# Zero-padded k heads and full-height score products, and a state sum on VectorE, in a linear-attention and MLP kernel

## The chip, the cores and the metric

One core of a Trainium2 chip runs the whole program. The engines are TensorE (PE, the matrix products; PEld is its weight load), VectorE (DVE), ScalarE (ACT), GpSimd (POOL) and SyncE (SP, which here only issues transfers). TensorE writes to PSUM[...]; VectorE and ScalarE read it from there. Everything else lies in SBUF, 128 partitions wide. Times are device microseconds of this core; the metric is the median of the runs.

## The reference

Four batches, 8 heads, 768 steps, head size 48. First a recurrent attention with a decay w per channel and a bonus u for the step itself, then an MLP with a norm and a residual:

```python
for t in range(S):
    cur = einsum('bhd,bhe->bhde', u * kt, vt)
    y[:, :, t] = einsum('bhd,bhde->bhe', rt, state + cur)
    state = w[..., None] * state + einsum('bhd,bhe->bhde', kt, vt)
x  = y as (B, S, H*D)                                   # 384 wide
xn = (x - mean) / sqrt(var + 1e-6) * g_ln
out = x + relu(xn @ w_ch1) @ w_ch2                      # 384 -> 1536 -> 384
```

## The kernel before

Each sequence of 768 steps is cut into six chunks of 128, so that there are 24 chunks, 6 to a batch, numbered 0 to 23. Within a chunk the recurrence is turned into products: k and r are scaled by powers of w (`scale_k`, line 359, and `scale_r`, line 362), k and r are transposed on TensorE (lines 377 and 392), and masked scores times v give the output of the chunk, to which the product of r with the state before the chunk is added. Heads are kept in pairs: a pair takes 128 partitions of a transposed tile, 64 to a head, of which 48 carry values and 16 are zeros.

For chunk i the steps are, with the planner's names:

- `TK` and `TR` transpose k and r into the PSUM bank `tr`, of which there is one (r for two chunks at a time). `kT` (line 381) and `rT` (line 398) copy them to SBUF as bf16, on ScalarE or VectorE.
- `q` (line 405) is the product of rT and kT for the bonus; `cc` (line 433) sums it over a head by four narrow matmuls into the last columns of the bank `s`; `cp` (line 444) copies the result, and `Vb` (line 448) multiplies v by it on GpSimd.
- `at` (line 412) is the scores: eight matmuls, one for each head, over 48 partitions, which begin at partition 0 for an even head and at 64 for an odd one. `A` (line 423) multiplies by the mask, in two instructions on VectorE that read PSUM.
- `kv` makes the new state in the bank `s`: an identity product adds the decayed state of the chunk before, Z (line 455), and four matmuls add k times v (line 464). `Z` (line 475) multiplies the sum by the decay of a whole chunk, on VectorE from PSUM, and writes bf16.
- `y` (lines 487 and 499) is r times Z and A times v. `x` (line 512) adds the bonus on VectorE, `xn` (line 525) and `sq` (line 532) on ScalarE prepare the norm, and `rs` (lines 538 and 541) on GpSimd makes the factor of the row, which is applied at the very end.
- xn is transposed for the MLP: on TensorE for chunks 0 to 7 (line 563), by DMA, issued on SyncE, for the others (`lc`, line 571).
- `up` (line 588) and `dn` (line 614) are the two MLP products, cut into blocks of some 0.65 us; `re` (line 599) is the relu on ScalarE; `ot` (line 624) finishes the row on VectorE, and `st` (line 635) stores it. The first six chunks go through the MLP singly, the others in pairs.

v comes as f32 and is cast to bf16 (`vc`, line 368) on whichever engine the plan gives it. The weights are scaled or cast once (lines 341, 343 and 353). Before the first down product, and only there, TensorE is kept busy with products of the identity (line 261).

The order of the work is not written out. A planner (`Planner.order`) holds for every step its engine, a cost, the steps it needs, the buffers it takes and gives back, a priority and, for some, other engines with their costs. It plays the program through with these costs, always takes the step that can start first, and picks the engine on which it would be done first. What comes out is a fixed order of instructions for each engine; on the chip each engine works through its own list and waits where an input isn't there. So a change of a cost, or of a buffer count, moves instructions on every engine. The pools are named in the call of the planner: `tr`, `at`, `s`, `y` and `o` are single PSUM banks, `hp` is two, and `x` has NX = 16 buffers in SBUF, each held from `x` to `ot`. Loads of k, v and r go through SyncE in a fixed row, with seven buffers for k and for v and four for r.

Of the kernel before, what the change touches and what calls it, by code (L numbers as in the profile page):

```python
# [9 lines left out]
FP32 = mybir.dt.float32  # L10
BF16 = mybir.dt.bfloat16
ALU = mybir.AluOpType
# [107 lines left out]
def kernel(  # L120
# [12 lines left out]
    nc = tc.nc  # L133
# [6 lines left out]
    DP = P // 2  # L140
# [10 lines left out]
    NX = 16  # L151
# [100 lines left out]
    nc.vector.memset(WLZ[:], 0.0)  # L252
    uwI = const.tile([P, HP, 2], BF16, name="uwI")
# [115 lines left out]

    def k_bank(i):  # L370
        return "y" if i < 1 else "tr"
# [7 lines left out]
    def evacuate_k(i, eng):  # L379
        kT_t[i] = trp.tile([P, HP, P], BF16, name="kT", bufs=NKT)  # L380
        (eng.copy if eng is nc.scalar else eng.tensor_copy)(out=kT_t[i][:], in_=tk_t[i][:, :HP, :])  # L381

# [20 lines left out]
    def product(i, eng):  # L403
        q_t[i] = sb2.tile([P, HP, P], BF16, name="q")
        eng.tensor_tensor(out=q_t[i][:], in0=rT_t[i][:], in1=kT_t[i][:], op=ALU.mult)  # L405

    def scores(i):
        at_t[i] = ps.tile([P, 2, HP, P], FP32, name="at")
        for p in range(HP):
            for par in range(2):  # L410
                p0 = par * DP
                nc.tensor.matmul(  # L412
                    out=at_t[i][:, par, p, :],
                    lhsT=kT_t[i][p0 : p0 + D, p, :],
                    rhs=rT_t[i][p0 : p0 + D, p, :],
                    start=True,
                    stop=True,
                )
# [33 lines left out]
    def state(i):  # L452
        ksc = k_bufs[i % NSC].rearrange("p (q e) d -> p q (e d)", e=2)
        if i % NCH > 0:
            nc.tensor.matmul(
                out=s_t[i][:, : HP * E2],
                lhsT=ident[:],
                rhs=Z_t[i - 1][:].rearrange("p q e -> p (q e)"),
                start=False,
                stop=True,  # L460
                skip_group_check=True,
            )
        for p in range(HP):
            nc.tensor.matmul(
                out=s_t[i][:, p * E2 : (p + 1) * E2],
                lhsT=ksc[:, p, :],
                rhs=v_t[i][:, 2 * p : 2 * p + 2, :],
                start=False,
                stop=True,
                skip_group_check=True,  # L470
            )

# [71 lines left out]
    xT_t, hT_t, o_t, rs_t = {}, {}, {}, {}  # L544
# [9 lines left out]
    KP = 24  # L554
    ot_t = {}
# [77 lines left out]
    def store(i, eng):  # L633
# [6 lines left out]
             Z=3, x=NX, sum=4, sqs=4, sq=2, xn=3, xT=3, hT=NH, ot=3)  # L640
# [42 lines left out]
    for i in range(NT):  # L683
# [17 lines left out]
        if i < KP:  # L701
# [8 lines left out]
        add(f"q{i}", "DVE", 0.45, lambda e, i=i: product(i, e), [f"kT{i}", f"rT{i}"], [("q", i, 1)], [("kT", i)], pri=p0 + 1, alt=[("POOL", 1.15)])  # L710
        add(f"at{i}", "PE", 0.43, lambda i=i: scores(i), [f"kT{i}", f"rT{i}"], [("at", i, 2)], [("kT", i)], pri=p0 + 1)
# [8 lines left out]
        if not last:  # L720
            z = [f"Z{i - 1}"] if c else []
            add(f"kv{i}", "PE", 0.36 if c else 0.2, lambda i=i: state(i), [f"cc{i}", f"vc{i}", f"sck{i}"] + z, [],
                [("sck", i), ("vv", i)] + ([("Z", i - 1)] if c else []), pri=p0 + 1)
            add(f"Z{i}", "DVE", 0.57, lambda i=i: decay(i), [f"kv{i}", "WLZ"],
                [("Z", i, 2 if c < NCH - 2 else 1)], [("s", i)], pri=p0)
# [35 lines left out]
    for t in plan.order():  # L761
# [5 lines left out]
        if t["fn"] is not None:  # L767
            if t["alt"]:
                t["fn"]({"ACT": nc.scalar, "DVE": nc.vector, "POOL": nc.gpsimd, "SP": nc.sync}[t["eng"]])
            else:  # L770
                t["fn"]()
# [28 lines left out]
```

## Time and profile before

| | |
|---|---|
| median of 6 runs | 163.03 us (162.03 to 164.77) |
| the profiled execution's time | 162.03 us |
| its span, first to last instruction | 160.0 us |
| first down product | 28.96 us |
| last x of the attention (line 512) | 121.16 us |
| TensorE busy | 149.6 us |
| VectorE busy | 108.6 us |
| ScalarE busy | 103.0 us |
| GpSimd busy | 87.0 us |
| input and output moved | 25.46 MB |

The span is 2.0 us shorter than the execution's time, and the profiled execution is the fastest of the six. Busy times are of one execution; an engine can be busy and still not set the end. In the lists of instructions, "x8" is eight equal instructions that follow each other, with the time from the start of the first to the end of the last; for TensorE that includes the time a product needs to run through, so that the next one starts before the printed end.

### The profile page before, as it was taken

The numbers are of one execution on the slowest core, as the hardware profiler recorded it, in microseconds if no ns is written. First come the engines' busy times: TensorE is split into PE (matmuls) and PEld (weight loads), VectorE is DVE, ScalarE is ACT, GpSimd is POOL, SyncE is SP. The second block draws the span as 40 slices with busy tenths as digits, with TensorE's granted clock in tenths as the row PEclk, the third lists the DMA queues.
The fourth block names the chain that finished last, engine by engine and source line by source line (L and its number), as shares of the span: only waits on it lengthen the run. The fifth ranks groups of instructions, "written<-read, shape, count | busy, mean of one in ns | idle before, by whom it ended". The sixth has DMA issues, their size and how long they took to land.

```text
span 160.0 us, 4708 instructions
## 1 busy us (share of the span) xinstructions
PE 149.6 (93%) x1875; PEld 117.1 (73%) x1875; DVE 108.6 (68%) x234; ACT 103.0 (64%) x234; POOL 87.0 (54%) x133
## 2 busy tenths in 40 slices
PE   5999999999999989999996979999999999999990
PEld 5788798787788757778874757878677777777550
DVE  5889997799887969889967967878693111111331
ACT  3575898788788697597929569676767554542000
POOL 7379897767489699969786943844152000000000
PEclk9999999999999999999999999999999999999998
DMA  4999999999999798999999862121121221101222
GB/s 101 222 229 333 346 197 296 360 209 233 228 232 251 151 256 166 247 236 171 233 163 209 158 161 74 53 63 39 49 49 53 74 74 49 50 3 51 102 104 87
DMA packets 75418, 25.46 MB, mean 159 GB/s; under 512 B 69632, under 2 KB 74246, under 8 KB 75398
## 3 DMA queue, kind: packets, MB, share of 16 engines
q1 hardware_dynamic: 73254, 23.60, 63.5%
q10 hardware_dynamic: 2048, 1.57, 3.0%
q8 instruction: 14, 0.23, 0.6%
q14 instruction: 6, 0.05, 0.1%
q0 software_dynamic: 96, 0.01, 0.0%
HBM read 18.88 MB, written 4.72 MB: 147 GB/s over the span
## 4 chain that ended last, share of the span: by engine, by line
PE 63%; SPq 13%; DMA 8%; ACT 7%; DVE 4%; issue 2%; ACTq 0%
PE hp L588 23%; PE o L614 23%; SPq L188 8%; DMA v<-in_v_dram 4%; DMA wst<-in_moe_w_ch_dram 4%; PE at L412 4%; PE tr L377 3%; SPq L182 2%; PE hp L614 2%; SPq L210 2%; PE tr L392 2%; PE y L499 2%; ACT hT L599 2%; ACT sq L532 2%; DVE A L423 2%
## 5 line engine op out<-in xcount | busy, mean ns | idle before, releaser
L588 PE MATMUL hp<-xT,w_sb 128*128 128x256 bf16 (+1 forms) x540 | 58.3, 251 | 2.9 <-ACT hT L599 1.3
L614 PE MATMUL o<-w_sb,hT 128*128 128x384 bf16 x264 | 52.6, 326 | 0.3 <-DVE ot L624 0.2
L599 ACT ACTIVATE hT<-hp 128x512 bf16<-128x512 f32 x72 | 42.1, 597 | 14.9 <-PE hp L588 13.7
L588 PEld LDWEIGHTS <-w_sb 128*128 128x128 bf16 x540 | 43.5, 98 | 10.4 <-issue 3.0
L614 PEld LDWEIGHTS <-hT 128*128 128x128 bf16 x288 | 26.9, 98 | 13.1 <-DVE w_sb L353 0.3
L624 DVE SCALAR_TENSOR_TENSOR ot<-o,rs,x 128x384 f32<-128x384 f32 x22 | 13.5, 613 | 28.4 <-PE o L614 28.4
L423 DVE TENSOR_TENSOR A<-at,mask 128x512 bf16<-128x512 f32 x48 | 30.7, 681 | 2.5 <-PE at L412 2.5
L448 POOL TENSOR_TENSOR Vb<-v,cc 128x384 f32<-128x384 f32 x24 | 21.4, 891 | 10.0 <-ACT cc L444 9.9
L362 POOL TENSOR_TENSOR sc<-r,Fr 128x384 bf16<-128x384 f32 x16 | 16.6, 1049 | 4.3 <-ACT Fr L303 2.7
L512 DVE SCALAR_TENSOR_TENSOR x<-y,Vb 128x384 f32<-128x384 f32 x24 | 13.2, 552 | 7.1 <-POOL Vb L448 4.9
L525 ACT ACTIVATE xn<-x,sum 128x384 bf16<-128x384 f32 x24 | 14.8, 615 | 4.5 <-DVE x L512 4.5
L359 POOL TENSOR_TENSOR sc<-k,Fk 128x384 bf16<-128x384 f32 x14 | 14.5, 1040 | 1.5 <-DMA k<-in_k_dram 1.3
L532 ACT ACTIVATE sq<-x,sum 128x384 bf16<-128x384 f32 x24 | 14.7, 613 | 0.0
L541 POOL TENSOR_TENSOR rs<-rs,expo 128x1 f32<-128x1 f32 x24 | 13.3, 555 | 2.0
L261 PE MATMUL o<-ident 128*128 128x128 bf16 x164 | 12.6, 232 | 1.6 <-DVE ident L236 1.6
L538 POOL TENSOR_SCALAR rs<-sqs 128x1 f32<-128x1 f32 x24 | 5.5, 231 | 12.9 <-ACT sq L532 9.0
L475 DVE TENSOR_TENSOR Z<-s,WLZ 128x384 bf16<-128x384 f32 x20 | 10.9, 547 | 2.3 <-ACT cc L444 2.3
L368 ACT CAST vv<-v 128x384 bf16<-128x384 f32 x14 | 7.2, 515 | 8.0 <-DMA v<-in_v_dram 8.0
L261 PEld LDWEIGHTS <-ident 128*128 128x128 bf16 x164 | 10.4, 104 | 2.0 <-DVE ident L236 1.6
L398 ACT COPY rT<-tr 128x512 bf16<-128x512 bf16 x12 | 8.6, 734 | 4.3 <-PE tr L392 2.9
L405 DVE TENSOR_TENSOR q<-rT,kT 128x512 bf16<-128x512 bf16 x22 | 10.6, 481 | 0.6 <-ACT kT L381 0.2
L377 PE MATMUL tr<-ident,sc 128*128 128x128 bf16 x92 | 8.9, 219 | 1.5 <-DVE rT L398 1.1
(81 smaller groups left out, 192.8 us busy)
## 6 DMA issues: line engine op xcount, KB each, us to landing
r<-in_r_dram SPq DMA_DIRECT2D x12, 384.0 KB, 4.8
k<-in_k_dram SPq DMA_DIRECT2D x24, 192.0 KB, 4.5
wst<-in_moe_w_ch_dram SPq DMA_DIRECT2D x6, 768.0 KB, 7.4
v<-in_v_dram SPq DMA_DIRECT2D x23, 192.0 KB, 3.9
out_dram<-ot SPq DMA_DIRECT2D x17, 192.0 KB, 2.0
out_dram<-ot ACTq DMA_DIRECT2D x7, 192.0 KB, 1.9
xT<-xn SPq DMA_TRANSPOSE x16, 3.0
v<-in_v_dram ACTq DMA_DIRECT2D x1, 192.0 KB, 3.8
```

Source lines behind the costliest of these rows:

```text
L261: nc.tensor.matmul(out=warm[:, :P], lhsT=ident[:], rhs=ident[:], start=True, stop=True)
L359: eng.tensor_tensor(out=k_bufs[i % NSC][:, :, :D], in0=k_t[i][:], in1=Fk[:], op=ALU.mult)
L362: eng.tensor_tensor(out=r_bufs[e % NSR][:, j, :, :D], in0=r_t[e][:, :, j * D : (j + 1) * D], in1=Fr[:, j], op=ALU.mult)
L377: nc.tensor.transpose(out=tk_t[i][:, q, :], in_=sc[:, q, :], identity=ident[:])
L423: nc.vector.tensor_tensor(out=A_t[i][:, par], in0=at_t[i][:, par], in1=mask[:].unsqueeze(1).to_broadcast([P, HP, P]), op=ALU.mult,)
L448: nc.gpsimd.tensor_tensor(out=Vb_t[i][:], in0=vf_t[i][:], in1=cc_t[i][:].unsqueeze(2).to_broadcast([P, H, D]), op=ALU.mult)
L525: nc.scalar.activation(out=xn_t[i][:], in_=x_t[i][:], func=ACT.Identity, bias=sum_t[i][:], scale=-float(C))
L532: nc.scalar.activation(out=sq[:], in_=x_t[i][:], func=ACT.Square, bias=sum_t[i][:], scale=-float(C), accum_out=sq_t[i][:])
L588: nc.tensor.matmul(out=hp[:, f * gw : (f + 1) * gw], lhsT=w1_sb[:, n, kc, fb * P : (fb + 1) * P], rhs=xT_t[g][:, kc, :gw], start=(kc == 0) ...
L599: nc.scalar.activation(out=hT_t[g][:, nf * m : nf * (m + 1), :gw], in_=hp_t[g, m][:].rearrange("p (f t) -> p f t", f=nf), func=ACT.Relu,)
L614: nc.tensor.matmul(out=o_t[i][:, :C], lhsT=hT_t[g][:, fk, j * P : (j + 1) * P], rhs=w2_sb[:, fk, :], start=(fk == 0), stop=(fk == FK - 1),)
L624: nc.vector.scalar_tensor_tensor(out=ot_t[i][:], in0=o_t[i][:, :C], scalar=rs_t[i][:], in1=x_t[i][:], op0=ALU.mult, op1=ALU.add,)
```

## The change

From chunk 8 on (KZ = 8) k is no longer copied to one SBUF tile. Three buffers of twice the size (kz) are zeroed once by GpSimd, and two copies, one for the even heads and one for the odd, put each head of k into its own 128-partition column, with zeros in the other head's half. The scores of these chunks are eight products over all 128 partitions. q reads k from the PSUM bank, which is given back only when both copies and q are done.

From chunk 6 on (SZ = 6), for chunks that are neither the first nor the last of their batch, the identity product is left out. VectorE adds the decayed state before to the k times v sum in PSUM and writes f32 (S, two buffers), and a second instruction multiplies this by the decay, on GpSimd or on VectorE as the planner picks. NX goes from 16 to 11. The planner's cost of the unpadded scores is 0.56 instead of 0.43.

```diff
-    NX = 16
+    NX = 11
@@
+    NKZ = 3
+    kz_bufs = []
+    for i in range(NKZ):
+        t_ = const.tile([P, HP, 2, P], BF16, name=f"kz{i}")
+        for par in range(2):
+            nc.gpsimd.memset(t_[(1 - par) * DP : (2 - par) * DP, :, par, :], 0.0)
+        kz_bufs.append(t_)
@@
+    def wide(i):
+        return KZ <= i < KP
@@
+    def spread_k(i, par, eng):
+        p0 = par * DP
+        (eng.copy if eng is nc.scalar else eng.tensor_copy)(
+            out=kz_bufs[i % NKZ][p0 : p0 + DP, :, par, :], in_=tk_t[i][p0 : p0 + DP, :HP, :]
+        )
@@ def product(i, eng):
-        eng.tensor_tensor(out=q_t[i][:], in0=rT_t[i][:], in1=kT_t[i][:], op=ALU.mult)
+        kT = tk_t[i][:, :HP, :] if wide(i) else kT_t[i][:]
+        eng.tensor_tensor(out=q_t[i][:], in0=rT_t[i][:], in1=kT, op=ALU.mult)
@@ def scores(i):
+        if wide(i):
+            for p in range(HP):
+                for par in range(2):
+                    nc.tensor.matmul(
+                        out=at_t[i][:, par, p, :],
+                        lhsT=kz_bufs[i % NKZ][:, p, par, :],
+                        rhs=rT_t[i][:, p, :],
+                        start=True,
+                        stop=True,
+                    )
+            return
@@ def state(i):
-        if i % NCH > 0:
+        if i % NCH > 0 and not apart(i):
@@
+    def apart(i):
+        return i >= SZ and 0 < i % NCH < NCH - 1
+
+    def add_state(i):
+        sum_s[i] = sb2.tile([P, HP, E2], FP32, name="S")
+        nc.vector.tensor_tensor(
+            out=sum_s[i][:],
+            in0=s_t[i][:, : HP * E2].rearrange("p (q e) -> p q e", q=HP),
+            in1=Z_t[i - 1][:],
+            op=ALU.add,
+        )
+
+    def decay_sum(i, eng):
+        Z_t[i] = sb3.tile([P, HP, E2], BF16, name="Z")
+        eng.tensor_tensor(out=Z_t[i][:], in0=sum_s[i][:], in1=WLZ[:], op=ALU.mult)
@@
+    KZ, SZ = 8, 6
@@ the plan
+        if wide(i):
+            add(f"TK{i}", "PE", 0.24, lambda i=i: transposes_k(i), [f"sck{i}"], [("tr", ("k", i), 3)], [("sck", i)], pri=p0)
+            add(f"kzb{i}", "", 0.0, None, [f"TK{i}"], [("kz", i, 1)], pri=p0)
+            for t in range(2):
+                add(f"kz{i}{t}", "ACT", 0.58, lambda g, i=i, t=t: spread_k(i, t, g), [f"kzb{i}"], [], [("tr", ("k", i))],
+                    pri=p0, alt=[("DVE", 0.45)])
+            add(f"kT{i}", "", 0.0, None, [f"kz{i}0", f"kz{i}1"], pri=p0)
...
+        if wide(i):
+            add(f"q{i}", "DVE", 0.55, lambda e, i=i: product(i, e), [f"TK{i}", f"rT{i}"], [("q", i, 1)], [("tr", ("k", i))],
+                pri=p0 + 1, alt=[])
+            add(f"at{i}", "PE", 0.45, lambda i=i: scores(i), [f"kT{i}", f"rT{i}"], [("at", i, 2)], [("kz", i)], pri=p0 + 1)
...
-        add(f"at{i}", "PE", 0.43, ...)
+            add(f"at{i}", "PE", 0.56, ...)
...
+            if apart(i):
+                add(f"kv{i}", "PE", 0.2, lambda i=i: state(i), [f"cc{i}", f"vc{i}", f"sck{i}"], [],
+                    [("sck", i), ("vv", i)], pri=p0 + 1)
+                add(f"S{i}", "DVE", 0.57, lambda i=i: add_state(i), [f"kv{i}"] + z, [("S", i, 1)],
+                    [("s", i), ("Z", i - 1)], pri=p0)
+                add(f"Z{i}", "POOL", 1.0, lambda e, i=i: decay_sum(i, e), [f"S{i}", "WLZ"],
+                    [("Z", i, 2 if c < NCH - 2 else 1)], [("S", i)], pri=p0 + 2, alt=[("DVE", 0.55)])
```

## The prediction

> **What bounds the kernel now.** I read the page's busy table and its 40 slices first: which engine is full, and where it is not.
>
> ```profile
> PE 149.6 (93%) x1875; PEld 117.1 (73%) x1875; DVE 108.6 (68%) x234; ACT 103.0 (64%) x234; POOL 87.0 (54%) x133
> PE   5999999999999989999996979999999999999990
> DVE  5889997799887969889967967878693111111331
> ACT  3575898788788697597929569676767554542000
> PEclk9999999999999999999999999999999999999998
> DMA  4999999999999798999999862121121221101222
> ```
>
> TensorE is full in nearly every 4 us slice and holds its full clock; the dips are slice 15 (56 to 60 us) and slices 22 and 24 (84 to 88 and 92 to 96 us). Inputs keep the DMA rings near full up to some 88 us. From 122 us on, only the MLP's products are left (DVE at 1). So: loads set the pace to 29 us, then TensorE with holes. To size the holes I costed TensorE's list after the first down product (starts 28.96 us) with start-to-start times from its timeline, because a printed duration there includes the pipeline's depth:
>
> ```profile
> 109.03 0.36 PE L499 MATMUL y<-vv,A 128*128 128x48 bf16 x8
> 109.32 0.40 PE L412 MATMUL at<-rT,kT 48*128 48x128 bf16 x8
> 109.65 0.25 PE L433 MATMUL s<-uwI,q 128*128 128x2 bf16 x4
> 109.76 0.32 PE L455 MATMUL s<-Z,ident 128*128 128x384 bf16 x1
> 109.92 0.33 PE L464 MATMUL s<-vv,sc 128*128 128x96 bf16 x4
> 110.09 0.61 PE L392 MATMUL tr<-ident,sc 128*128 128x128 bf16 x8
> 110.54 0.81 PE L614 MATMUL o<-w_sb,hT 128*128 128x384 bf16 x4
> ```
>
> Scores take 0.33, then bonus 0.11, identity product 0.16, state 0.17, eight full-height transposes 0.45. Before the scores stands a hole: eight y products take 0.20 (as from 49.36 to 49.57), so 109.23 to 109.32 is about 0.10 lost, and the same hole precedes almost every set of scores. A set costs 0.43. With 0.65 for a down or up block, 0.37 for y and 0.22 for a k transpose, 72 down, 65 up, 20 scores, 20 bonus, 13 identity, 16 state, 20 y, 19 k, 9 r and 5 LayerNorm transposes sum to 121.0 us: the end would be 150.0. TensorE really ends at 156.3. **6.3 us are holes**: 0.9 by chunk 7's y, 2.7 by chunk 15's, 4.6 by chunk 17's, 6.0 by chunk 18's, 6.3 at the end. The chain of waits names the two large ones:
>
> ```profile
> 80.08 3.68 DMA v<-in_v_dram
> 83.78 0.02 ACT vv L368
> ...
> 89.88 3.25 DMA v<-in_v_dram
> 93.16 0.02 ACT vv L368
> ```
>
> ScalarE stood at a v cast (line 368) whose load SyncE issued late, behind a DMA transpose waiting for xn; the relu behind it held an up block.
>
> **The change on TensorE.** Twelve identity products go (chunks 7 to 10, 13 to 16, 19 to 22): 12 x 0.163 = -1.96 us. Sixteen sets of scores become full height. Here a rule speaks against the change: the Trainium skill, "TensorEngine Tiling (Array Packing)", Theoretical Speedup, gives up to 2x for a contraction of at most 64, so padding could double a set. The row says 0.33 for eight, 41 ns each, against 56 ns for a full-height transpose of the same width: packing earns a quarter. The same page (Key Properties) says that a change of tiling mode drains the array; the 0.10 hole is where that would stand, and uniform height should remove it. By the 2x rule, with no hole charged, a set goes from 0.22 to 0.44 (+3.6 us over 16). By the rows 0.43 becomes 8 x 0.0555 = 0.44: +0.2 us. I take the rows. If the hole stays, 16 x 0.10 = +1.6; if the printed 0.40 were a set's real length, -0.9. Net TensorE: -1.75 us.
>
> The built program's order also moves 1.7 us of work (an up block, chunk 4's scores, bonus, state and one LayerNorm transpose) in front of the first down product, where TensorE now runs filler. After it stand 117.55 us.
>
> **The change on the other engines**, durations from these rows, less some 0.08 where the timeline shows the next start earlier:
>
> ```profile
> L455 PE MATMUL s<-Z,ident 128*128 128x384 bf16 x16 | 5.2, 323 | 0.0
> L423 DVE TENSOR_TENSOR A<-at,mask 128x512 bf16<-128x512 f32 x48 | 30.7, 681 | 2.5 <-PE at L412 2.5
> L475 DVE TENSOR_TENSOR Z<-s,WLZ 128x384 bf16<-128x384 f32 x20 | 10.9, 547 | 2.3 <-ACT cc L444 2.3
> L405 DVE TENSOR_TENSOR q<-rT,kT 128x512 bf16<-128x512 bf16 x22 | 10.6, 481 | 0.6 <-ACT kT L381 0.2
> L381 ACT COPY kT<-tr 128x512 bf16<-128x512 bf16 x17 | 9.9, 585 | 0.5 <-PE tr L377 0.3
> L381 DVE COPY kT<-tr 128x512 bf16<-128x512 bf16 x6 | 2.5, 418 | 0.7 <-PE tr L377 0.7
> ```
>
> - k spread: two copies per chunk instead of one, each over half the partitions but the same 512 elements, so no cheaper: 0.42 on VectorE, 0.58 on ScalarE (half of it at best, the full row at worst; I take the full row). 22 land on ScalarE, 10 on VectorE.
> - q now reads k from PSUM. By its own row it stays at 0.43; the skill's "VectorE: DVE Perf Modes" (perf-mode tier table) allows a two-tensor operation 2x only from bf16 SBUF and 1x with any PSUM operand. The mask row, 512 elements from PSUM, takes 0.68. I take 0.60 start to start: +0.2 x 16 = 3.2 us; by q's row 0.
> - State sum: like the Z row, 0.50. Of the 12 decays, the order leaves 7 on VectorE. Both inputs are now f32 SBUF as in k scaling, 0.74 (0.50 if like Z). Five go to GpSimd at about 1.0, the k-scaling row there (0.83 by the Vb row); it has 46% free.
> - The tr bank is held until both spreads and q are done, some 1.2 us after the transpose against 0.6. What queues behind it on TensorE is the next r, k or LayerNorm transpose; 2.2 us or more of products lie between in the order, so I charge nothing. The scores, which wait for both spreads, stand 1.4 us or more behind the k transpose. Cover gone, it is 0.6 a chunk, 10 us at the most.
> - Six half-height memsets on GpSimd follow its row-DMA issues at 3.7 us, in a 2.67 us wait for Fr: 0.2 us each (the mask's memset, 128 elements) to 0.5 (one element takes 0.10, so 512 some 0.10 + 4 x 0.10), 1.2 to 3.0 in all, zero to 0.4 late on work that loads hide until 29 us.
> - NX 11: VectorE's order lets x run 8 to 9 chunks ahead of the finished output instead of 11, so attention is spread to about 127 us instead of 121; nothing waits for a slot that its own order has not freed.
>
> **VectorE between chunk 7's x and chunk 23's** (50.7 to 121.6 us: 58.6 busy, 12.4 idle). The same stretch of the new order: 32 masks x 0.60, 16 x's x 0.56, 16 q x 0.60, 10 spreads x 0.42, 11 sums x 0.50, 9 decays 6.2, 13 ot x 0.55, 6 rT x 0.66, 7 r scalings x 0.75, two more 1.1: 71.3 us. TensorE's sum for it is 77.1.
>
> **Holes in the new order.** The first down product needs two casts that now follow each other on GpSimd (28.57 + 2 x 0.69 = 29.95): +0.9. Loads come no earlier: r3 landed at 35.1, v7 at 38.7; chunk 6's work now comes earlier in TensorE's order, and v7's cast stands on VectorE ahead of chunk 6's rT: holes 2.2 in all by then, so most of the 1.7 moved forward is lost again. v11's cast (issue 47.02, median landing 3.9) stands on ScalarE right behind v10's: +0.8. The DMA transpose for chunk 9 stands two DMA issues later on SyncE: landing near 67, +1.3. The late v loads have 3 to 4 us more slack, since attention is later: I drop those 3.2 us. For small holes that I can't place I take the 2.7 that before shows by chunk 15. Sum 7.0. By VectorE instead, 71.3 plus the old 12.4 idle exceeds 77.1 by 6.6, and with 2.2 that is 8.8. I take 7.75 between them: TensorE ends at 29.0 + 117.55 + 7.75 = 154.3, that is 2.0 us earlier.
>
> That is 158.0 span against 160.0, 160.0 us against the profiled 162.03. The profiled run was the fastest of the six; from the median 163.03 it is **161.0 us**. A difference under 1% (1.6 us) can hardly be told from no change here.
>
> **Rivals.**
> - **VectorE becomes the bound** (slower). Before, it idles 0.77 us a chunk in that stretch. The gain is gone when the holes reach 156.3 - 146.55 = 9.75; less 2.2, the stretch then lasts 77.1 + 7.55 = 84.65, and 84.65 - 71.3 is 0.83 idle a chunk. At 1.0 it lasts 87.3, the holes are 12.4, TensorE ends at 158.95, 2.65 late: 165.7 us. For it: the state now goes from VectorE to GpSimd and back, and the tr bank, the spreads and q are one chain. Against: behind each state sum the s bank's next user stands over 1 us later in the order, and two of the old idle pieces (1.2 and 1.6 us) are those behind v loads.
> - **The v stalls vanish and the small holes too**: holes 4.7, -3.05 more: 158.0. For: those loads' slack; against: VectorE's 71.3.
> - **The hole before the scores stays**, so full height costs what packing saved: 161.0 + 1.5 = 162.5.
>
> **How the numbers follow.** Forecast 0.48 (its own range 159 to 163.2; of it 0.32 faster, 0.16 same), VectorE-bound 0.30 (0.26 slower, 0.04 same), fewer holes 0.12 (faster), hole stays 0.10 (0.08 same, 0.02 slower). Faster 0.44, same 0.28, slower 0.28. Range 158.0 to 166.3: half of the best case and the worst part of VectorE's are left out.
>
> **What the changed profile would show.** Scores at full height near 0.44 for eight with no hole ahead; 4 identity products; q from PSUM near 0.65 and spreads near 0.42 and 0.58; VectorE over 85% busy from 51 us to the last x; no v wait of 2 us on ScalarE near 80 to 95 us; the last x near 127 us. I am wrong if k transposes wait for the tr bank, if VectorE's idle in that stretch passes 14 us, or if a q at 0.43 leaves VectorE free.

## The result, and the profile after

| | before | changed |
|---|---|---|
| median | 163.68 us (161.64 to 166.16, 72 runs) | 162.38 us (160.89 to 164.79, 35 runs) |
| ratio to before | | 0.9952, 95% interval 0.993 to 0.9973 |
| the profiled execution's time | 162.03 us | 162.74 us |
| its span | 160.0 us | 161.0 us |
| first down product | 28.96 us | 30.98 us |
| last x of the attention | 121.16 us | 131.87 us |

The forecast was 161.0 us from a median of 163.03, 1.25% less. Measured is 0.48% less: the right sign, inside the range, and under half of the forecast gain. The medians here are over all runs and by themselves 0.8% apart; every ratio and interval in this document leaves out the slow runs, those over 1.5% above the fastest of their kernel. The two traces stand the other way round (161.0 us of span against 160.0), because before's profiled execution was one of its fastest and that of the changed kernel is an ordinary one. A step of less than 1.5 us is therefore not read off these two traces alone below.

The busy table of the changed kernel and three of its rows of 40 slices, 4 us each:

```profile
PE 147.5 (92%) x1841; PEld 118.5 (74%) x1841; DVE 114.8 (71%) x247; ACT 110.1 (68%) x245; POOL 92.8 (58%) x143
PE   5879999999899997979996999999999999999990
DVE  5889999997789867997855988978875781101131
DMA  4999979996998979889699762412202212111122
```

TensorE is 2.1 us less busy, and the span is no shorter: the time went into holes. The dips in PE are spread from the second slice on, where before had three places. VectorE works on the attention until about 132 us instead of 121 (forecast: 127), at 79% (64.3 of the 80.9 us from 51.0 to 131.9; forecast: over 85%). It isn't as full as forecast.

The new parts, one set of products each, on TensorE's timeline (start, duration, instruction), and by groups (busy us, mean ns of one, idle time before them). Here as in all listings below, `<-` behind an idle time names what ended it:

```profile
118.47 0.36 PE L545 MATMUL y<-vv,A 128*128 128x48 bf16 x8
118.67 0.61 PE L430 MATMUL at<-rT,kz 128*128 128x128 bf16 x8
119.11 0.24 PE L462 MATMUL s<-uwI,q 128*128 128x2 bf16 x4
119.22 0.33 PE L493 MATMUL s<-vv,sc 128*128 128x96 bf16 x4
```

```profile
L396 ACT COPY kz<-tr 64x512 bf16<-64x512 bf16 x22 | 12.7, 578 | 3.1 <-DVE q L423 1.9 <-PE tr L387 1.0
L423 DVE TENSOR_TENSOR q<-rT,tr 128x512 bf16<-128x512 bf16 x16 | 6.7, 416 | 5.0 <-ACT kz L396 2.9 <-PE tr L387 1.6
L508 DVE TENSOR_TENSOR S<-s,Z 128x384 f32<-128x384 f32 x12 | 6.6, 549 | 0.6 <-ACT cc L473 0.5
L517 POOL TENSOR_TENSOR Z<-S,WLZ 128x384 bf16<-128x384 f32 x5 | 5.3, 1064 | 0.1
L258 POOL MEMSET kz<- 64x512 bf16 x6 | 3.1, 518 | 0.2
```

The scores follow the y products after 0.20 us, without a hole, and take 0.44 (118.67 to 119.11). The identity product is gone: 0.11 after the bonus begins, the state does. Spreads, S and the decays have nearly the forecast durations. q from PSUM takes 0.42 and not 0.60, but VectorE stands 2.9 us before it for a ScalarE copy that q doesn't read.

How the holes gather, by the forecast's own bookkeeping (TensorE's list costed start to start from 29.0 us, subtracted from where the y products of a chunk really start):

| us of holes at the y of chunk | 4 | 7 | 10 | 13 | 15 | 17 | 23 |
|---|---|---|---|---|---|---|---|
| before | 0.2 | 0.9 | 2.1 | 2.6 | 2.8 | 4.6 | 6.1 |
| changed | 2.0 | 4.1 | 6.3 | 7.5 | 9.5 | 9.8 | 10.4 |
| changed, another run | 2.0 | 3.6 | 5.3 | 6.4 | 8.9 | 9.2 | 9.8 |

Forecast were 2.2 by chunk 7 and 7.75 at the end. Two places can be read at once. At the start, GpSimd's line in the changed kernel, then VectorE's, changed and before:

```profile
3.78 3.31 POOL L258 MEMSET kz<- 64x512 bf16 x6
7.07 0.98 POOL L369 TENSOR_TENSOR sc<-r,Fr 128x384 bf16<-128x384 f32 x1
8.02 0.98 POOL L366 TENSOR_TENSOR sc<-k,Fk 128x384 bf16<-128x384 f32 x1
```

```profile
6.73 2.69 DVE L366 TENSOR_TENSOR sc<-k,Fk 128x384 bf16<-128x384 f32 x1 [0.20 <-ACT Fk L310]
6.73 1.08 DVE L359 TENSOR_TENSOR sc<-k,Fk 128x384 bf16<-128x384 f32 x1 [0.20 <-ACT Fk L303]
```

The clearing of kz ends at 7.07 and two scalings follow it on GpSimd without a gap, to 9.00. VectorE's first scaling of k, begun at 6.73, ends at 9.42, 0.42 after the last of them: 2.69 us, where before it took 1.08 from the same 6.73. The first down product is 2.0 us later, not 0.9; it starts at 30.98 to 31.02 in six of the seven traces that have the clearing at the start (30.19 in the seventh, the one with zero products below). The second place is at chunk 15; three engines' lines:

```profile
86.87 0.51 ACT L375 CAST vv<-v 128x384 bf16<-128x384 f32 x1 [1.33 <-DMA v<-in_v_dram]
87.28 0.57 ACT L396 COPY kz<-tr 64x512 bf16<-64x512 bf16 x1
```

```profile
87.89 0.42 DVE L423 TENSOR_TENSOR q<-rT,tr 128x512 bf16<-128x512 bf16 x1 [1.86 <-ACT kz L396]
```

```profile
88.37 0.25 PE L462 MATMUL s<-uwI,q 128*128 128x2 bf16 x4 [1.30 <-ACT hT L646]
```

ScalarE stands 1.33 us at a v cast; the kz copy queued behind it is late; VectorE's q, whose inputs had been there since about 84.8 us, waits 1.86 us for that copy. The readers of one PSUM tile follow each other: of the 30 neighbouring pairs of kz copies and q's that stand on different engines in this trace, none overlap. TensorE's bonus then waits 1.30 us for q, which ends at 88.31 (the releaser named is only the last semaphore to come; the weight load beside it waits 1.7 us, for q by name). So the stall on late v loads, which the forecast let go, was still there, by a new road.

### The profile page after: what moved, and what is told of

Same layout as the page of the kernel before. It is cut to its first block, busy times and chain, and to the rows that moved or that the text cites. A ratio compares the mean times of both kernels' runs of the same rounds, so it can differ in the third digit from the quotient of the medians.

```text
span 161.0 us, 4696 instructions
## 1 busy us (share of the span) xinstructions
PE 147.5 (92%) x1841; PEld 118.5 (74%) x1841; DVE 114.8 (71%) x247; ACT 110.1 (68%) x245; POOL 92.8 (58%) x143
## 4 chain that ended last, share of the span: by engine, by line
PE 58%; DMA 10%; SPq 8%; DVE 8%; POOL 6%; ACT 6%; issue 2%; DVEq 0%; POOLq 0%
PE hp L635 20%; PE o L661 18%; DMA v<-in_v_dram 7%; SPq L188 5%; PE at L430 4%; DMA xT<-xn 3%; PE hp L661 2%; PE o L268 2%; PE tr L387 2%; SPq L182 2%; POOL sc L366 2%; POOL Vb L477 2%; DVE sc L366 2%; PE s L493 2%; PE tr L409 1%
## 5 line engine op out<-in xcount | busy, mean ns | idle before, releaser
L661 PE MATMUL o<-w_sb,hT 128*128 128x384 bf16 x264 | 53.3, 326 | 0.5 <-DVE ot L671 0.5
L477 POOL TENSOR_TENSOR Vb<-v,cc 128x384 f32<-128x384 f32 x24 | 20.5, 855 | 10.2 <-ACT cc L473 9.6
L366 POOL TENSOR_TENSOR sc<-k,Fk 128x384 bf16<-128x384 f32 x19 | 20.0, 1051 | 8.1 <-PE s L493 6.3
L396 ACT COPY kz<-tr 64x512 bf16<-64x512 bf16 x22 | 12.7, 578 | 3.1 <-DVE q L423 1.9
L415 ACT COPY rT<-tr 128x512 bf16<-128x512 bf16 x14 | 10.2, 730 | 4.8 <-DVE rT L415 2.8
L369 POOL TENSOR_TENSOR sc<-r,Fr 128x384 bf16<-128x384 f32 x12 | 12.3, 1030 | 2.0 <-PE tr L610 2.0
L268 PE MATMUL o<-ident 128*128 128x128 bf16 x142 | 11.2, 234 | 1.6 <-DVE ident L236 1.6
L430 PE MATMUL at<-rT,kz 128*128 128x128 bf16 x128 | 10.4, 219 | 0.5 <-ACT kz L396 0.3
L268 PEld LDWEIGHTS <-ident 128*128 128x128 bf16 x142 | 9.2, 105 | 1.9 <-DVE ident L236 1.6
L423 DVE TENSOR_TENSOR q<-rT,tr 128x512 bf16<-128x512 bf16 x16 | 6.7, 416 | 5.0 <-ACT kz L396 2.9
```

What stands on the lines that cost most here:

```text
L268: nc.tensor.matmul(out=warm[:, :P], lhsT=ident[:], rhs=ident[:], start=True, stop=True)
L366: eng.tensor_tensor(out=k_bufs[i % NSC][:, :, :D], in0=k_t[i][:], in1=Fk[:], op=ALU.mult)
L430: nc.tensor.matmul(out=at_t[i][:, par, p, :], lhsT=kz_bufs[i % NKZ][:, p, par, :], rhs=rT_t[i][:, p, :], start=True, stop=True,)
L477: nc.gpsimd.tensor_tensor(out=Vb_t[i][:], in0=vf_t[i][:], in1=cc_t[i][:].unsqueeze(2).to_broadcast([P, H, D]), op=ALU.mult)
L661: nc.tensor.matmul(out=o_t[i][:, :C], lhsT=hT_t[g][:, fk, j * P : (j + 1) * P], rhs=w2_sb[:, fk, :], start=(fk == 0), stop=(fk == FK - 1),)
```

## Experiments

Ratios are to the kernel before, run in turn on the same chip. The expectations name their theories in words.

### The start

The changed kernel again, and the same with the clearing of kz moved into GpSimd's later waits, just ahead of three named steps:

> The changed kernel as it is, beside the experiments on the same chip, so that each of them has its own reference. Expected: ratio to the kernel before 0.993 to 0.998, as on record.

```diff
-            nc.gpsimd.memset(t_[(1 - par) * DP : (2 - par) * DP, :, par, :], 0.0)
+    clear_at = {"w2s00": [(0, 0), (0, 1)], "w2s10": [(1, 0), (1, 1)], "scr30": [(2, 0), (2, 1)]}
@@ for each step t of the plan
+        for i, par in clear_at.get(t["name"], []):
+            clear_kz(i, par)
```

> The six GpSimd memsets of the padded k buffers no longer stand at the start but in three places of GpSimd's list where its trace shows it waiting (before the first casts of w_ch2 at 27.6 and 29.6 us, and before the scaling of r for chunk 6 at 34.4 us); every other instruction keeps its place. Theory A (the memsets push GpSimd's first scaling of r onto VectorE's first scaling of k, which took 2.69 us instead of 1.08, and the whole attention starts 1.5 us late, which the first down product, 30.98 against 28.96, still shows): first k scaling back near 1.1 us, first down product at 29.5 to 30.0, 1.0 to 1.5 us faster than the changed kernel, ratio to the kernel before about 0.987. Rival B (the loads hide the start, as forecast): within 0.3 us of the changed kernel.

Measured: 161.68 us, ratio 0.9899 (0.9862 to 0.9935), and 161.28 us, 0.9879 (0.9824 to 0.9935). The late clearing does what it should where it was made, on VectorE's line:

```profile
7.26 0.83 DVE L369 TENSOR_TENSOR sc<-k,Fk 128x384 bf16<-128x384 f32 x1 [0.72 <-ACT Fk L313]
```

The first down product comes at 29.81 instead of 31.01. Yet the holes are 4.4 at chunk 8 and 5.3 at chunk 10, against 4.5 and 5.3. Most of the 1.2 us is gone even by chunk 7: 3.4 to 3.6 us of holes in three traces with late clearing, 3.5 to 4.1 in four with the clearing at the start. Something else sets the pace there. The ratios can't say what is left at the end: their intervals have room for nothing and for the whole 1.2 us.

### The products

> The changed kernel, its order untouched, with the TensorE time of the twelve removed identity products put back: three identity products of 128 zero columns each, 0.17 us a chunk, which wait for nothing and add zeros. If TensorE's own work sets the end (as the forecast has it), it is 1.7 to 2.0 us slower than the changed kernel, ratio to before about 1.006. If holes swallow the saving, because the end is set by loads, ScalarE and VectorE until 96 us, it is under 0.7 us slower.

```diff
+        if apart(i):                       # products of the identity with zeros, into the state's bank
+            for n in range(HP * E2 // P):
+                nc.tensor.matmul(out=s_t[i][:, n * P : (n + 1) * P], lhsT=ident[:],
+                                 rhs=k_bufs[i % NSC][:, :, D:DP], start=False, stop=True, ...)
```

163.58 us, ratio 0.9896 (0.9813 to 0.9978). The ratio rests on two of the six runs and can't tell 1.96 us from nothing. The question stays open.

> The changed kernel with the scores of chunks 8 and up again over 48 partitions, even heads from partition 0 and odd ones from 64, but read from the padded tiles, so that only the height of the 128 products changes and nothing else moves. By the rows (0.33 and a hole of 0.10 against 0.44) it is the same as the changed kernel within 0.3 us. If the hole is dearer than it looks (the planner's new 0.56 against 0.45), it is 1.8 us slower; if packing pays, up to 1.6 us faster.

```diff
-                        lhsT=kz_bufs[i % NKZ][:, p, par, :],
-                        rhs=rT_t[i][:, p, :],
+                        lhsT=kz_bufs[i % NKZ][par * DP : par * DP + D, p, par, :],
+                        rhs=rT_t[i][par * DP : par * DP + D, p, :],
```

161.61 us, 0.9894 (0.9852 to 0.9936). Half height on the padded tiles, on the same timeline:

```profile
117.42 0.36 PE L545 MATMUL y<-vv,A 128*128 128x48 bf16 x8
117.71 0.40 PE L430 MATMUL at<-rT,kz 48*128 48x128 bf16 x8
118.04 0.25 PE L462 MATMUL s<-uwI,q 128*128 128x2 bf16 x4
```

The hole of 0.09 is back ahead of the scores (117.62 to 117.71), and the set is at 0.33: 0.42 against 0.44. Height by itself makes no difference that can be measured here, as forecast.

### Where a microsecond of TensorE counts

The same zero products, 2.66 us in all, in chunks 7 to 10 or in chunks 19 to 22:

```diff
+        if 7 <= i <= 10:                   # or 19 <= i <= 22
+            for n in range(4 * (HP * E2 // P)):
+                ...                        # the zero product of above
```

> The changed kernel with twelve products of 128 zero columns added ahead of the state products of each of chunks 7, 8, 9 and 10 (12 x 0.0555 = 0.67 us a chunk, 2.66 us in all, between 45 and 65 us); nothing else moves. Theory A (up to some 90 us the arrival of k, v and r sets the pace, and TensorE's holes swallow work added or saved there): less than 0.9 us slower than the changed kernel. Rival B (TensorE sets the pace throughout, holes are a constant): 2.7 us slower.

> The same 2.66 us of zero products, in chunks 19 to 22 instead (between 108 and 127 us). By both theories 2.4 to 2.7 us slower than the changed kernel; it gives the scale for the early ones. If less than 1 us, the end isn't TensorE's at all.

Early: 163.09 us, 1.0015 (0.9967 to 1.0062). Late: 164.85 us, 1.012 (1.004 to 1.02). The same work costs 1.7 us more where it is late. What of it is left at the end, against the changed kernel, depends on which of its ratios is taken (0.9952 or 0.9899, neither measured beside these two): 1.0 to 1.9 us of the early 2.66, 2.7 to 3.6 of the late. By the holes, with the added products counted among them, the early ones stand at 11.0 at the end against 9.8 to 10.4 without. So until about 90 us, where the loads end, a part of an early microsecond is swallowed.

### The loads out of the way

k and v are loaded as contiguous runs of 1,536 bytes instead of 192. The bytes, the issues and the lists of instructions are the same; k's and v's values stand in other places, in these and in all later kernels with long runs.

```diff
-        eng.dma_start(out=dst[:], in_=src[b, :, s0 : s0 + L, :].rearrange("h t d -> t h d"))
+        run = src[b].rearrange("h t d -> (h t d)")[c * L * C : (c + 1) * L * C]
+        eng.dma_start(out=dst[:].rearrange("p h d -> p (h d)"), in_=run.rearrange("(p f) -> p f", p=P))
```

> The changed kernel, but each k and v load takes a contiguous block of the same size, 1536 bytes for a partition instead of eight pieces of 192 bytes; so values stand in other places than in the reference, and bytes, tiles, order and work stay. Theory A (loads set the pace to 90 us): 3 to 6 us faster than the changed kernel, and the holes up to chunk 16, 9 us now, shrink below 6. Rival C (the holes are those of ScalarE's and VectorE's fixed lists): less than 1 us faster.

> The kernel before with the same contiguous loads of k and v (values in other places than in the reference, the same bytes and work). Theory A: it gains less than the changed kernel does, since its holes are 6 us and not 10, so that the changed kernel's lead grows from some 1 us to 2.5 us or more, near the 3.4 us that its TensorE list is shorter by behind the first down product. Rival C: the lead stays near 1 us.

Changed: 158.66 us, 0.972 (0.9652 to 0.9788). Before: 157.35 us, 0.9661 (0.9587 to 0.9735). The loads are still there, but nothing waits for them: in neither trace does an engine wait 0.2 us or more for a load between 30 and 95 us. PE and DMA slices of the changed kernel with long runs, then PE of before with them:

```profile
PE   5989999998999999989999999999999999999990
DMA  4999999914893877786993421311202121011122
```

```profile
PE   5999999999999999999999999999999999999990
```

Before then has 1.6 us of holes in all, the changed kernel 6.3 (4.1 of them by chunk 7). **With the loads fast the change loses 1.3 us** between the medians, 1.0 by the ratios; one of its four runs falls among those of before. The list after the first down product is shorter by 3.44, and the holes are longer by 4.7: 1.26 together, as measured. So the holes of the changed kernel are mostly made by its own lists, and those of before mostly by loads. The expectation that the lead would grow with fast loads fell. Turned round: the loads cost before 5.5 us (1 - 0.9661 of 163) and the changed kernel 2.9 (0.9899 - 0.972, same chip) to 3.8 (from 0.9952). Each of these ratios has an interval of about 0.7%, 1.2 us. That is where its gain comes from: the loads hurt it less.

### Which part makes the lists' holes

Four kernels with long runs: late clearing; the state split alone; the padding alone; and the order alone, which is the kernel before with one number of the plan changed. The first three are made from the changed kernel and so have its NX = 11 too, the order alone has 16; what NX is worth by itself no run shows.

```diff
-        add(f"at{i}", "PE", 0.43, lambda i=i: scores(i), ...)     # y4, and z1 below: before, with
+        add(f"at{i}", "PE", 0.56, lambda i=i: scores(i), ...)
@@
-    KZ, SZ = 8, 6
+    KZ, SZ = 24, 6         # y2, z4: split alone, nothing cleared
+    KZ, SZ = 8, 24         # y3, z5: padding alone, late clearing
```

> The changed kernel with the clearing of the padded k tiles moved to GpSimd's later waits, and with k and v loaded as contiguous runs of 1,536 bytes (k and v values stand in other places than in the reference, so the output values differ; the work is the same). The two loads-out-of-the-way kernels stood at 0.972 (changed) and 0.966 (before) of the kernel before; a step of 0.006 is 1 us. With short runs the late clearing brought the first down product 1.2 us earlier and the end nothing. Theory (without the loads' pace behind it, an early loss is kept to the end): 1.2 us earlier than the changed kernel with long runs, 0.9645 of the kernel before, 157.3 us, holes at the end 5.1 against 6.3. Rival (the order of the attention chain sets the pace there, and takes the 1.2 us back by chunk 7): 0.972, holes at the end 6.3.

> The state sum and decay taken off TensorE from chunk 6 on, as in the change, with k padded nowhere (half-height scores, one k copy a chunk, q from SBUF, no clearing of tiles), long runs for k and v (their values stand in other places than in the reference). Theory (the split costs the small late holes: the state passes VectorE and GpSimd and back): it saves 12 identity products, 1.96 us, and pays 1 us or more in holes, so 0.960 to 0.967 of the kernel before, 156.5 to 157.6. Rival (the split is free and the padding carries the cost): the whole 1.96 us is seen against the kernel before with long runs and the planner's cost of a set of scores at 0.56, which runs beside it.

> The padded k tiles and full-height scores from chunk 8 on, as in the change, with late clearing, and the state summed on TensorE in every chunk as before; long runs for k and v (their values stand in other places than in the reference). Theory (padding carries the holes: the tr bank's readers follow each other on two engines, VectorE has 3 us more work): slower than the kernel before with long runs (0.966) by 1 us or more, 0.972 to 0.980, 158.5 to 159.8. Rival (padding is paid for by the hole ahead of the scores): within 0.5 us of 0.966.

> The kernel before with one number changed, the planner's cost of a set of scores, 0.43 to 0.56 as in the change (there for chunks 0 to 7, here for all), and long runs for k and v (their values stand in other places than in the reference). The written order then moves chunk 4's scores and an up block ahead of the first down product, as the change does; no instruction is added or taken away. Theory (the new order by itself brings the 0.9 us at the first down product less the clearing, and the 1.7 to 2.1 us by chunk 7): slower than 0.966 by 0.5 to 1.5 us, 0.969 to 0.975. Rival (the order follows from nothing that costs time): 0.966 within 0.002.

| long runs | median us | ratio (95%) | list after the first down product | holes at its start, at chunk 7, at the end |
|---|---|---|---|---|
| before (e7) | 157.35 | 0.9661 (0.9587 to 0.9735) | 121.0 | 0.3, 0.4, 1.6 |
| order alone (y4) | 158.06 | 0.9701 (0.9654 to 0.9749) | 119.3 | 1.2, 3.3, 3.9 |
| order and split (y2) | 158.94 | 0.9765 (0.972 to 0.9809) | 117.35 | 0.9, 3.0, 6.5 |
| order and padding (y3) | 160.05 | 0.9834 (0.9781 to 0.9886) | 119.5 | 0.7, 2.9, 5.8 |
| all, late clearing (y1) | 157.56 | 0.9682 (0.9637 to 0.9727) | 117.55 | 0.7, 2.9, 5.2 |
| all, early clearing (e6) | 158.66 | 0.972 (0.9652 to 0.9788) | 117.55 | 2.0, 4.1, 6.3 |

Here list and holes add up to the medians within 0.4 us, so the steps can be read in order. The order by itself moves 1.7 us forward and pays 2.3 in holes for it, all of them there by chunk 7. All parts together save 1.75 more and pay 1.3. Clearing at the start costs 1.1, and with fast loads nothing gives it back. But the two parts don't add: each alone, on top of the order, costs 0.9 and 2.0 us (more than was expected of either), and both together gain 0.5, which is not clear of noise. One reason can be seen in VectorE's q (minimum, median and maximum ns), first of y2, then of y1:

```profile
L424 DVE TENSOR_TENSOR q<-rT,kT x21: 424/677/1218, 9.7 to 114.6; 128x512 bf16<-128x512 bf16 x21
```

```profile
L427 DVE TENSOR_TENSOR q<-rT,tr x16: 408/421/422, 50.2 to 123.2; 128x512 bf16<-128x512 bf16 x16
L427 DVE TENSOR_TENSOR q<-rT,kT x8: 426/747/1123, 9.5 to 43.7; 128x512 bf16<-128x512 bf16 x8
```

With both inputs in SBUF q takes anything up to 1.2 us; with k in PSUM it takes 0.42, always. In the changed kernel's own trace each of the five q's over 0.43 us overlaps an operation of GpSimd, and eleven of the sixteen with k in PSUM overlap one too and take no longer. The Trainium skill ("SBUF — State Buffer", SBUF: two separate sides) says that a VectorE operation with two SBUF inputs and a GpSimd operation that reads SBUF exclude each other on a pair of ports for a whole instruction. These rows agree. The scaling of 2.69 us fits only in part: VectorE was the first to begin (6.73, GpSimd's scalings from 7.07) and yet ended 0.42 after the second of them; why it did not get in sooner is not shown. What TensorE waits for q in the stretch from 28 to 85 us (total us, times, longest), in y2, then in y1:

```profile
PE s L463 <- DVE q L424: 1.3, 4, 0.4
```

```profile
PE s L466 <- DVE q L427: 0.4, 1, 0.4
```

That is 0.9 of the 1.3 us of holes between them. In the same list y2 also waits 0.7 for a scaling of k on GpSimd and 0.4 more for a copy of rT.

The padding alone (y3) has q in PSUM, so its 2.0 us have another cause. One place shows it; TensorE's line and two of VectorE's:

```profile
52.22 0.33 PE L614 MATMUL tr<-ident,xn 128*128 128x128 bf16 x3 [0.61 <-ACT hT L650]
50.68 0.41 DVE L427 TENSOR_TENSOR q<-rT,tr 128x512 bf16<-128x512 bf16 x1
51.73 0.43 DVE L400 COPY kz<-tr 64x512 bf16<-64x512 bf16 x1 [0.64 <-ACT kz L400]
```

The three readers of chunk 8's k, q, a copy on ScalarE (51.12 to 51.70) and a copy on VectorE, follow each other until 52.16, and the next transpose into the bank `tr` starts 0.06 later, 0.61 us after TensorE was free for it. This is the bank that the forecast charged nothing for. Its other holes were not traced.

### The same square with the real loads

> The kernel before with one number changed: the planner's cost of a set of scores, 0.43 to 0.56 (in the change for chunks 0 to 7, here for all). No instruction is added or taken away; chunk 4's scores, bonus and state and an up block move ahead of the first down product. With long runs this order cost 0.7 us. Theory (the loads set the pace to some 90 us, so early holes are swallowed): 0.998 to 1.002 of the kernel before. Rival (the order's cost is seen with real loads too): 1.004, 0.7 us slower.

> The state sum and decay taken off TensorE from chunk 6 on, as in the change, with half-height scores and unpadded k throughout (no clearing of tiles). With long runs its holes between chunk 8 and 13 made it 0.9 us slower than the order alone. Theory (with real loads those holes lie where loads set the pace, and the identity products taken out after 90 us, 8 of 12, are seen): 0.990 to 0.994 of the kernel before. Rival (its holes add to those of the loads): 1.003 to 1.010.

> The padded k tiles and full-height scores from chunk 8 on with late clearing, the new order at the start (0.56), and the state summed on TensorE in every chunk as before; real loads. The order alone stood at 1.017, the order with the state split at 0.993. With long runs the padding cost 2.0 us on top of the order. Theory (TensorE carries 2 us more than in the changed kernel and none of the holes go): 1.000 or more of the kernel before, up to 1.01. Rival (the order alone was slow by one stall on a late v load, which any other plan moves): 0.990 to 0.999.

> The changed kernel with late clearing and its own order, again. It stood at 0.988 (0.982 to 0.994); the same with the old order at 0.995 (0.990 to 1.000). Theory (in the changed kernel the new order is worth its 1.7 us moved forward): 0.986 to 0.990 again. Rival (the two are one value, and 0.988 was a low draw): 0.992 to 0.995.

A part of z4's output is wrong, which is not intended; the cause stays open. It and y2, its twin with long runs, carry the split's whole list of instructions, and only their times are used. If the cause were a wait that is missing, these times would be too short.

| real loads | median us | ratio (95%) | holes at the end |
|---|---|---|---|
| order alone (z1) | 166.52 | 1.0166 (1.0097 to 1.0235) | 12.7 |
| order and split (z4) | 163.31 | 0.9932 (0.9873 to 0.9991) | 9.8 |
| order and padding (z5) | 162.27 | 0.9972 (0.9935 to 1.0008) | 8.1 |
| all, late clearing (e1, and again) | 161.28, 161.36 | 0.9879 (0.9824 to 0.9935), 0.9902 (0.9869 to 0.9935) | 9.9, 7.8 |

The order alone costs 2.7 us, four times what it costs with long runs; "loads swallow it" fell, and so did the rival's 0.7. Three of its 12.7 us stand in one place. From the chain of waits of z1 (start, duration, what), and TensorE's line at its end:

```profile
79.25 4.59 DMA v<-in_v_dram
83.84 0.05 issue
83.89 0.50 POOL vv L368
...
85.27 0.84 POOL Vb L448
86.11 0.02 issue
86.14 0.04 DVE x L512
86.17 0.45 issue
86.62 0.08 DVE x L512
86.70 0.65 DVE q L405
```

```profile
87.39 0.25 PE L433 MATMUL s<-uwI,q 128*128 128x2 bf16 x4 [2.89 <-DVE q L405]
```

A v load of 4.6 us, its cast on GpSimd, the bonus value Vb, x on VectorE, and the q that is queued behind x: TensorE stands 2.89 us. Each part of the change, laid over this order, gives back 3 to 4 us; as work the split saves 1.95 of TensorE and the padding nothing. That they do it by moving or shortening this stall fits their holes (no step of more than 1.4 us at chunk 15 or 16 in either, against 3.0 in z1), but no run isolates it, so that a part is worth here what it does to the late v loads is argued and not shown.

### The old order

The changed kernel with late clearing, and the plan's cost of the half-height scores back at 0.43, so that the order at the start is that of before:

> The changed kernel with the planner's cost of a half-height set of scores (chunks 0 to 7) back at 0.43, so that TensorE's order around the first down product is that of before, and with the late clearing of the padded tiles. Theory (loads swallow the order): as the late-clearing run, 0.988 of the kernel before. Rival (the order is the lost part of the forecast): 0.983 to 0.985, 0.7 us better, holes at the end near 8 against the larger remaining list of 119.2 us.

> The same as the old-order run, with k and v loaded as contiguous runs of 1,536 bytes (k and v values stand in other places than in the reference). Theory (the order's cost adds up with the rest): 0.7 us better than the late-clearing kernel with long runs (0.968), that is 0.964, 156.9 us, and better than the kernel before with long runs (0.966) by 0.4 us. Rival (each order that the planner writes has its own small holes, and the parts don't add up): anywhere from 0.962 to 0.975; a value above 0.970 speaks for this one.

With real loads 163.5 us, 0.995 (0.99 to 1.0001); with long runs 159.01 us, 0.9712 (0.9636 to 0.9788), where 0.964 was expected if things added up. Going back is no gain. By the ratios the new order, which costs the kernel before 0.7 us with long runs, is worth 0.5 us to the changed one with long runs and 0.8 to 1.2 with real loads, all within the intervals. Each order that the planner writes has its own small holes.

With real loads the changed kernel with late clearing has the lowest ratios, 0.988 and 0.990. On the one chip where both ran, the changed kernel itself stood at 0.990, so the late clearing is not told apart from it with real loads.

## Why the prediction was right in sign and wrong in size

**The list: right.** 12 identity products and 1.7 us moved forward left 117.55 us after the first down product; a set of full-height scores is 0.44, and the hole ahead of it went. The factor of up to two that the prediction cites for a short contraction was not reached here (0.33 and the hole of 0.09, against 0.44); the row decided. The rival "the hole stays" fell, and at half height on the same tiles the hole was back.

**The holes: this is the step that failed.** The forecast had 7.75 us of them at the end; the two traces have 10.4 and 9.8. Of the 2.1 to 2.6 us that are missing in the forecast, 1.4 to 1.9 are there by chunk 7 (forecast 2.2, measured 4.1 and 3.6), before the wide scores and all but one of the removed identity products come. Most of it is the new order: the kernel with the order alone has 3.3 by chunk 7, with the real loads and with long runs alike. The memsets add some 0.3 there with the real loads.

In the forecast's sum, the lists' own part grew by 2.2 (the new order), lost 0.4 that were dropped, and got an allowance of 0.75 for VectorE: 2.55. The loads' part fell by 1.1 (3.2 dropped, 0.8 and 1.3 added). With the loads fast the lists' part grew by 4.7: 2.3 from the order; 1.1 from the memsets, priced at nothing; 1.3 from split and padding. The loads' part fell by 1.7 to 2.6 (5.5 against 3.8 to 2.9), more than forecast. The two errors are of opposite sign, so a part of the miss is hidden. Taken together, 4.7 less some 2.1 is 2.6 us of holes more, and 3.44 - 2.6 leaves 0.8 us. That this is the measured 0.48% is no test of it, since the loads' part was got from the same four times; and it takes lists and loads as if they added, which they do only roughly, as the square with the real loads shows.

**The memsets: the term "zero to 0.4 late on work that loads hide until 29 us" failed.** They take 0.52 each, their sum of 3.1 is just over the top of the range named (1.2 to 3.0), and they put the first down product 1.2 us later. That work was not hidden by loads until 29 us. With the loads fast the 1.1 us are paid in full to the end; with the real loads most of the 1.2 is swallowed by chunk 7.

**The new order: too small, and for the wrong reason.** The first down product 0.9 to 1.0 later without the memsets (29.81 to 30.01 in five traces, 28.96 before) is as forecast. The rest of the 2.2 was put down to loads that come no earlier. But with long runs no engine waits 0.2 us or more for a load between 30 and 95 us, and the order alone still has 3.3 us of holes by chunk 7 against 0.4. Between the first down product and 42 us TensorE stops at the same four places with long runs and with the real loads, 1.6 and 1.8 us in all. Two of them, first with long runs (y4), then with the real loads (z1):

```profile
35.59 0.81 PE L615 MATMUL o<-w_sb,hT 128*128 128x384 bf16 x4 [0.25 <-DVE ot L625]
40.66 0.33 PE L564 MATMUL tr<-ident,xn 128*128 128x128 bf16 x3 [0.28 <-ACT rT L399]
```

```profile
36.10 0.81 PE L614 MATMUL o<-w_sb,hT 128*128 128x384 bf16 x4 [0.25 <-DVE ot L624]
41.16 0.33 PE L563 MATMUL tr<-ident,xn 128*128 128x128 bf16 x3 [0.27 <-ACT rT L398]
```

So the lists make these holes, and not the loads. It fits that TensorE reaches these steps sooner in the new order, while VectorE and ScalarE are not done with what comes before them.

**q from PSUM: wrong, to the good side.** 0.60 was taken by the perf-mode rule that the prediction cites; measured is 0.416, as q's own row gave it, and the measurement decides. The 3.2 us of VectorE time were never spent. The spreads (0.42 and 0.58) and S (0.55 printed, 0.50 forecast start to start) were right; the decay on VectorE is 0.66, not 0.74.

**VectorE as the bound: two signs of being wrong came true.** Its idle time in the stretch is 16.6 us, over the 14 named and near the 1.0 a chunk of that rival, and a q of 0.42 leaves VectorE at 79%. The rival's end (165.7 us) did not come with it, because VectorE had 64.3 us to do and not 71.3.

**"I drop those 3.2": right in its result, wrong in its reason.** From chunk 15 to chunk 18 before loses 3.2 us and the changed kernel 0.5. But the waits for v did not go away, and the stall at chunk 15 (1.30 us; 1.5 in the other trace) is new. All waits at v casts between 30 and 95 us, first before, then changed (total us, times, longest):

```profile
ACT vv L368 <- DMA v<-in_v_dram: 7.5, 6, 2.5
POOL vv L368 <- DMA v<-in_v_dram: 3.0, 3, 1.4
DVE vv L368 <- DMA v<-in_v_dram: 0.3, 1, 0.3
```

```profile
POOL vv L375 <- DMA v<-in_v_dram: 6.9, 4, 2.2
ACT vv L375 <- DMA v<-in_v_dram: 5.9, 7, 1.4
DVE vv L375 <- DMA v<-in_v_dram: 0.8, 1, 0.8
```

10.8 us became 13.6; in three more traces of the changed kernel, two of them with late clearing, they are 11.9, 12.8 and 7.4, so they neither grew nor shrank for certain. About half of them now stand on GpSimd. What is left on ScalarE reaches TensorE through the kz copy and q.

**The tr bank: the kind of trouble named, in other places.** One transpose of k waits 0.9 us for the bank, but behind a copy of rT, as one did before (0.8); none waits for the spreads and q. What queues in the changed kernel is the readers: q waits 2.9 us for ScalarE's copies and ScalarE 1.9 us for q, though neither needs the other's result. With the padding alone a LayerNorm transpose does stand for them (0.61 us).

**The transpose by DMA for chunk 9: right in kind.** Forecast as a wait of 1.3 us near 67 us; TensorE waited 0.74 for it, ending at 70.1.

## What to carry to other kernels

When the holes of a kernel are what matters, find out first who makes them: lay the loads out in long runs, so that the lists stay as they are and nothing waits for a transfer, and see which holes are left. An edit that moves a planner's cost is two edits, the work and the order, and the order alone cost the kernel before 0.7 to 2.7 us here, so it deserves its own run. A clearing placed in a wait of GpSimd is not free by that alone: look at what it pushes back in GpSimd's queue, and at what VectorE reads from SBUF beside that (2.69 us against 1.08 here).

## What was not expected of the hardware

VectorE's product of two bf16 tiles took 0.407 to 0.422 us with one of them in PSUM, in all 16 cases, and 0.407 to 1.126 with both in SBUF, for the same 512 elements. Chunks 8 to 23 took 416 ns on the mean with k in PSUM, and 477 in the kernel before with k in SBUF, so moving an operand to PSUM made q steadier and a little faster. Runs of 192 bytes against 1,536 bytes, of the same bytes in the same transfers, cost the kernel before 5.5 us and the changed one 2.9 to 3.8. Eight products of 48 partitions, which start in pairs some 2 to 5 ns apart, took 0.33 us and a hole of 0.09 ahead; eight of 128 partitions took 0.44: the packed form saved 0.02.
